# First softmax's weights of five sequences: transposed by VectorE in 32x32 blocks and by transfers within SBUF, in place of TensorE

## The chip, the core and the metric

One core of a Trainium2 chip runs the whole program. A core has TensorE (PE: matrix products, and transposes as products with an identity matrix), VectorE (DVE), ScalarE (ACT) and GpSimd (POOL). Each of them, and SyncE (SP), which in this kernel issues every transfer, works through a program of its own in a fixed order, and semaphores make one wait for another. Sixteen DMA engines move the data. Operands lie in SBUF, which has 128 partitions; products come out in the eight banks of PSUM. The metric is the time of one execution on the device, in microseconds (us).

## The reference

Eight sequences (B=8) of 576 positions, with eight heads of 64 elements, go through two softmax attentions by way of 32 packed rows for each head, and then through a channel mix with d_model = 512 and d_ff = 1024:

```python
p_packed = sm_attn(p, k, v)             # weights: 32 x 576 for each head
out = sm_attn(q, p_packed, p_packed)    # weights: 576 x 32
x = out.transpose(0, 2, 1, 3).reshape(B, S, H * D)
xk = mu_k * x + (1.0 - mu_k) * x_prev   # x_prev: the position before
xr = mu_r * x + (1.0 - mu_r) * x_prev
k = np.maximum(xk @ w_k, 0.0)
v = k * k @ w_v
r = 1.0 / (1.0 + np.exp(-(xr @ w_r)))
return r * v
```

All of it is float32. The first softmax's weights, p against k, come out with the 4 x 32 packed rows of four heads on the partitions and the 576 positions along the free axis. For the product with v the positions have to lie on the partitions, so these weights must be transposed. That step is what the change is about.

## The kernel before, in words

**Channel mix.** The 4608 rows are taken in nine blocks of 512. Each block has 48 products for the gate (`gates`, L862 to L864), 96 for the keys (`keys`, L822 to L824) and 96 for the values (`values`, L891 to L893), each 128 x 128 by 512. The operands are split into a high and a low part, so that three products stand for one. These 2160 products form the bulk of TensorE's work.

**Attention** of the sequences runs in the gaps of the channel mix, about one sequence ahead of the block that needs it. For a sequence b, `front(b)` multiplies p by k (L465, "the scores"), and `weights_of` takes each half h of the heads (0 or 1) through the first softmax: the maximum on VectorE (L540), its scaled negative (L542), and the exponential on ScalarE (L546) into the tile `a`. Five transposes on TensorE (four at L556, one at L557) turn `a` into a PSUM bank of the pool `pa`, and ScalarE copies the bank to `aT` in SBUF (L562, L564). Then `front` multiplies with v (L489, twenty products for each half; this document calls them the products with v), normalises on VectorE (L504), and `back` does the second softmax on VectorE and ScalarE and the product at L632. `mixed_in` and `mix` make the channel mix's operands of it.

**Buffers.** There is one slot for `aT`, so the second half can't write its weights before the first half's products with v are done. `e` has two slots, which `back` uses for the second softmax. `vt` has two slots for v. Before, v's first 512 positions lie in `vt` and the last 64 in `vl`. `raw` has three slots for q and k as they come in, and `kq` has four for their transposed form.

**What sets the order.** Each of these steps is a generator. `Flow` holds a planned time for every engine; each step states its engine and an estimated cost, and `Flow.run` always takes the step that can start first by the plan, then the one of better rank. That decides the order of the instructions on every engine when the program is built. On the chip nothing is moved any more: an engine whose next instruction isn't ready waits, and what stands behind it waits too. The plan's transfers are `load`: an issue on the queue (SP), a time on the DMA engines, and `LANDS` = 2.0 until the data may be used. From the third sequence on (b of 2 and more) q and k come in with position t*18 + tb in column tb*32 + t, for VectorE's 32x32 block transposes (L366). The sequences are b = 0 to 7; the change touches b = 3 to 7.

Of the kernel before, what the change touches and what calls it, by code (L numbers as in the profile page):

```python
# [8 lines left out]
F32 = mybir.dt.float32  # L9
# [154 lines left out]
def attn_pack_channel_mix(ctx: ExitStack, tc: tile.TileContext, q, k, v, p, mu_k, mu_r, w_k, w_v, w_r, out):  # L164
    nc = tc.nc
    B, H, S, D = q.shape
    NP = p.shape[2]
    DM, DF = w_k.shape
    P = 128
    NG = H // 4  # L170
    NPR = H // 2
    HS = S // 2
    NTB = S // 32
    NQ = 4 * P
# [9 lines left out]
    flow = Flow()  # L184
# [5 lines left out]
    def vec(n, after=None):  # L190
        return "vector", 0.07 + 1.04e-3 * n, after, None
# [4 lines left out]
    def act(n, after=None, table=None):  # L196
        return "scalar", 0.14 + 0.72e-3 * n, after, table
# [4 lines left out]
    def pe(us, after=None):  # L202
        return "tensor", us, after, None

    def load(dst, src, issue, us):
        yield "queue", issue, None, None
        nc.sync.dma_start(dst, src)
        begin = max(flow.free.get("dma", 0.0), flow.t + 0.46)
        flow.free["dma"] = begin + us
        flow.free["queue"] = max(flow.free["queue"], begin - 2.0)  # L210
        flow.now.t = begin + us + LANDS
# [5 lines left out]
    def reached():  # L217

        yield None, 0.0, None, None

    EARLY = 2

    const = ctx.enter_context(tc.tile_pool(name="const", bufs=1))
# [8 lines left out]
    def tile_(shape, dtype, tag, slot, name=None):  # L232
        return sb.tile(shape, dtype, name=name or tag, tag=f"{tag}{slot}")

    def banks(slot):
        return ps.tile([P, 2, 512], F32, name="pa", tag=f"pa{slot}")
# [5 lines left out]
            const.tile([P, 1 if "m" == tag[0] or "n" == tag[0] else 2], F32, name=f"{tag}{j}", tag=f"{tag}{j}")  # L242
    for tag, n, size in (
        ("xk", NC, 2 * TB), ("sq", NF, 2 * TB), ("tmp", 4, WP), ("sig", 4, DM), ("kq", 4, S), ("a", 2, S),
        ("raw", 3, S), ("a2", 1, S), ("e", 2, S), ("aT", 1, 5 * P), ("vt", 2, NPR * 4 * D),
    ):
        for j in range(n):
            sb.tile([P, size], F32, name=tag, tag=f"{tag}{j}")
# [51 lines left out]
    ts, vts, pts, xts, xt2 = {}, {}, {}, {}, {}  # L300

    def rank(b, n=0):

        return (10 if b == 0 else RANK_1 if b == 1 else 30) + 0.1 * (2 * b + n)
# [4 lines left out]
    def loads(b):  # L309
        flow.spawn(packed(b), lrank(b) - (0.03 if b else 0.015))  # L310
        for src, tag in ((k, "kT"), (v, "vt"), (q, "qT")):
# [8 lines left out]
            for pr in range(NPR):  # L320

                space = "xk" if b == 0 else "raw"
                slot = yield from flow.take(space)
                if b < EARLY:

# [21 lines left out]
    def back_to_issue():  # L347
        flow.now.t = flow.free["queue"]

    def values_of(b, h):  # L350

        slot = yield from flow.take("vt")
        vt = tile_([P, NPR, 4 * D], F32, "vt", slot)
        vl = tile_([S - NQ, NPR, D], F32, "vl", slot)
        yield from load(vt, v[b, h::2, :NQ, :].rearrange("h (p c) d -> p h (c d)", c=4), 0.46, 1.8)
        back_to_issue()
        yield from load(vl, v[b, h::2, NQ:, :].rearrange("h p d -> p h d"), 0.63, 0.45)
        vts[b, h] = slot, vt, vl
        flow.set(("vt", b, h))

    def transposed(tag, b, pr, raw_slot, raw):
# [86 lines left out]
    def two_slots():  # L448

        lock = yield from flow.take("both")  # L450
        first = yield from flow.take("pa")
        second = yield from flow.take("pa")
        flow.give("both", lock)
        return first, second

    def front(b):

        yield from flow.wait(("pt", b), *(("kT", b, pr) for pr in range(NPR)))
        slots = yield from two_slots()
        yield pe(1.2)  # L460
        s1 = [banks(slot) for slot in slots]
        for hf in range(2):
            for pr in range(NPR):
                for h, own in enumerate(HALVES):
                    nc.tensor.matmul(  # L465
                        s1[h][32 * pr:32 * pr + 32, hf, :HS], pts[b][1][own, pr, :],
                        ts["kT", b, pr][1][own, hf * HS:(hf + 1) * HS],
                        start=True, stop=True,
                    )
        for pr in range(NPR):  # L470
            flow.give("kq", ts.pop(("kT", b, pr))[0])
        flow.give("pt", pts.pop(b)[0])
        sm = const.tile([P, 2], F32, name="sm", tag=f"sm{b % 2}")
        for h in range(2):
            flow.spawn(weights_of(b, h, slots[h], s1[h], sm), rank(b) + 0.01 * h)

        yield from flow.wait(("aT", b, 0))
        slot = yield from flow.take("pa")
        pv = banks(slot)
        for h in range(2):  # L480
            yield from flow.wait(("aT", b, h), ("vt", b, h))
            yield pe(0.55)
            sv, vt, vl = vts.pop((b, h))
            sT, aT = aTs.pop((b, h))
            for c in range(5):
                n = P if c < 4 else S - NQ
                for pr in range(NPR):
                    own = slice(32 * pr, 32 * pr + 32)
                    nc.tensor.matmul(  # L489
                        pv[own, h, :D], aT[:n, c, own], vt[:, pr, c * D:(c + 1) * D] if c < 4 else vl[:, pr, :],  # L490
                        start=(c == 0), stop=(c == 4),
                    )
            flow.give("aT", sT)
            flow.give("vt", sv)
        summed = flow.t
        rs = const.tile([P, 2], F32, name="rs", tag=f"rs{b % 2}")
        yield vec(2, after=0.0)
        nc.vector.tensor_scalar_add(rs, sm, eps)
        yield vec(20)
        nc.vector.reciprocal(rs, rs)  # L500
        sp = yield from flow.take("pm")
        pm = tile_([P, 2, D], F32, "pm", sp)
        yield vec(P, after=max(flow.t, summed))
        nc.vector.tensor_tensor(pm, pv[:, :, :D], rs.unsqueeze(2).broadcast_to([P, 2, D]), op=ALU.mult)  # L504
        flow.give("pa", slot)

        slot = yield from flow.take("pa")
        yield pe(0.21)
        pT = banks(slot).rearrange("p a b -> p (a b)")
        nc.tensor.transpose(pT[:, :P], pm.rearrange("p a b -> p (a b)"), ident)  # L510
        ppT = sb.tile([P, P], F32, name="ppT", tag="ppT")
        yield act(P)
        nc.scalar.copy(ppT, pT[:, :P])
        flow.give("pa", slot)
        left = [2]
        first = None
        if b == 0:
            sx = yield from flow.take("xt")

            a2 = tile_([P, 2, S + 1], F32, "xt", sx, "a2t")  # L520
            nc.gpsimd.memset(a2[:, :, 0:1], 0.0)
            first = dict(a2=(sx, a2), left=4)
            flow.spawn(shared(ppT, first), RANK_MIX - 0.1)
        for hf in range(2):
            flow.spawn(back(b, hf, sp, pm, ppT, left, first), rank(b, hf) - 1)

    aTs = {}

    def in_order(b, natural, blocks, x):

        if b < EARLY:
            return natural, x[:, :, :HS]
        return blocks, x[:, :, :HS].rearrange("p a (b t) -> p a b t", t=32)

    def weights_of(b, h, slot, s1, sm):

        mx = const.tile([P, 1], F32, name="mx", tag=f"mx{h}")
        nmx = const.tile([P, 1], F32, name="nmx", tag=f"nmx{h}")
        yield vec(S)
        nc.vector.tensor_reduce(mx, s1[:, :, :HS], axis=AX.XY, op=ALU.max)  # L540
        yield vec(1)
        nc.vector.tensor_scalar_mul(nmx, mx, -scale)  # L542
        sa = yield from flow.take("a")
        a = tile_([P, S], F32, "a", sa)
        yield act(S + 320 if b < EARLY else 2 * S + 220, table="exp")
        nc.scalar.activation(  # L546
            *in_order(b, a.rearrange("p (a s) -> p a s", a=2), a.rearrange("p (t a b) -> p a b t", a=2, t=32), s1),
            AF.Exp, bias=nmx, scale=scale, accum_out=sm[:, h:h + 1],
        )
        flow.give("pa", slot)  # L550

        slot = yield from flow.take("pa")
        yield pe(0.65)
        tp = banks(slot).rearrange("p a b -> p (a b)")
        for c in range(4):
            nc.tensor.transpose(tp[:, c * P:(c + 1) * P], a[:, c:NQ:4], ident)  # L556
        nc.tensor.transpose(tp[:S - NQ, NQ:NQ + P], a[:, NQ:], ident)  # L557
        flow.give("a", sa)
        sT = yield from flow.take("aT")
        aT = tile_([P, 5, P], F32, "aT", sT)  # L560
        yield act(NQ)
        nc.scalar.copy(aT[:, :4, :], tp[:, :NQ].rearrange("p (a b) -> p a b", b=P))  # L562
        yield act(P, after=0.0)
        nc.scalar.copy(aT[:S - NQ, 4, :], tp[:S - NQ, NQ:NQ + P])  # L564
        flow.give("pa", slot)
        aTs[b, h] = sT, aT
        flow.set(("aT", b, h))

# [74 lines left out]
    def mixed_in(b, hf, g, slot, px):  # L643
# [8 lines left out]
        xt = xt2[b, g][1]  # L652
        yield act(S if b < EARLY else 2 * S)
        nc.scalar.copy(*in_order(
# [334 lines left out]
```

## Time and profile before

| | |
|---|---|
| three executions | 603.91, 605.03, 605.74 us; median 605.03 us |
| the profiled execution | 605.65 us, of which the span from its first to its last instruction is 603.9 us |
| matrix products for the weights' transposes of b = 3 to 7 | 50 of TensorE's instructions in the program |
| ScalarE's copy of the transposed weights, L562 and L564 | 586 ns and 256 ns, for each half of each sequence |
| VectorE's 32x32 block transpose of a 128 x 576 tile, L366 | 754 to 765 ns |
| transfers issued by SP | 354 |

The profile's page gives for each engine the busy time, then the span in 40 slices, the queues, the chain of work that ended last, and groups of instructions by line. A matrix product's duration is the time that it spends in a pipeline; successive products overlap, so the distance between the starts of two of them says what one costs, and the duration doesn't. The trace counts a float32 product of the attention twice (two passes), so that L465's 16 products appear as x32.

### The profile page before, as it was taken

The numbers are of one execution on the slowest core, as the hardware profiler recorded it, in microseconds if no ns is written. First come the engines' busy times: TensorE is split into PE (matmuls) and PEld (weight loads), VectorE is DVE, ScalarE is ACT, GpSimd is POOL, SyncE is SP. The second block draws the span as 40 slices with busy tenths as digits, with TensorE's granted clock in tenths as the row PEclk, the third lists the DMA queues.
The fourth block names the chain that finished last, engine by engine and source line by source line (L and its number), as shares of the span: only waits on it lengthen the run. The fifth ranks groups of instructions, "written<-read, shape, count | busy, mean of one in ns | idle before, by whom it ended". The sixth has DMA issues, their size and how long they took to land.

```text
span 603.9 us, 10289 instructions
## 1 busy us (share of the span) xinstructions
PE 592.3 (98%) x4024; PEld 466.1 (77%) x4024; DVE 361.8 (60%) x702; ACT 324.5 (54%) x578; POOL 2.1 (0%) x22
## 2 busy tenths in 40 slices
PE   8899999999999999999999999999999999999997
PEld 8675777777777777777877787778788888888886
DVE  2499989949688489456856576267403812541321
ACT  4457793775674758454945484458434703631410
POOL 0000000000000000000000000000000000000000
PEclk9899999999999999999999999999999999999999
DMA  8679560765535645446034602000000010001001
GB/s 235 170 216 297 179 146 3 177 120 120 88 50 150 106 76 117 116 77 139 2 101 75 137 0 78 13 1 0 35 37 0 1 71 1 0 1 69 1 1 69
DMA packets 159312, 49.43 MB, mean 82 GB/s; under 512 B 143904, under 2 KB 152096, under 8 KB 159264
## 3 DMA queue, kind: packets, MB, share of 16 engines
q1 hardware_dynamic: 159264, 48.79, 33.8%
q8 instruction: 31, 0.51, 0.3%
q14 instruction: 17, 0.14, 0.1%
HBM read 39.33 MB, written 9.44 MB: 81 GB/s over the span
## 4 chain that ended last, share of the span: by engine, by line
PE 86%; DVE 5%; ACT 3%; DMA 3%; issue 1%; SPq 1%
PE pvo L891 11%; PE ph L822 11%; PE pvo L892 10%; PE pvo L893 10%; PE ph L823 10%; PE ph L824 10%; PE pr L862 5%; PE pr L863 5%; PE pr L864 5%; PE pa L489 2%; PE pa L577 2%; PE pa L632 2%; DMA vt<-in_v 1%; PE pa L465 1%; PE pa L556 1%
## 5 line engine op out<-in xcount | busy, mean ns | idle before, releaser
L822 PE MATMUL ph<-xk,wk_h 128*128 128x512 f32 x288 | 115.0, 399 | 0.0
L891 PE MATMUL pvo<-wv_h,sq 128*128 128x512 f32 x288 | 113.9, 396 | 0.0
L823 PE MATMUL ph<-xk,wk_h 128*128 128x512 f32 x288 | 112.7, 391 | 1.1 <-DVE xk L729 1.1
L824 PE MATMUL ph<-xk,wk_l 128*128 128x512 f32 x288 | 112.4, 390 | 0.0
L892 PE MATMUL pvo<-wv_l,sq 128*128 128x512 f32 x288 | 112.3, 390 | 0.0
L893 PE MATMUL pvo<-wv_h,sq 128*128 128x512 f32 x288 | 112.2, 390 | 0.0
L840 DVE CAST sq<-r 128x512 fp32r<-128x512 f32 x72 | 30.2, 420 | 99.2 <-ACT r L836 98.6
L833 ACT ACTIVATE r<-ph 128x512 f32<-128x512 f32 x72 | 43.0, 597 | 86.7 <-PE ph L824 85.8
L822 PEld LDWEIGHTS ph<-xk,wk_h 128*128 128x128 f32 x288 | 54.1, 188 | 16.1 <-issue 4.5
L891 PEld LDWEIGHTS pvo<-wv_h,sq 128*128 128x128 f32 x288 | 54.1, 188 | 16.0 <-issue 4.5
L823 PEld LDWEIGHTS ph<-xk,wk_h 128*128 128x128 f32 x288 | 54.2, 188 | 12.4 <-DVE xk L729 2.3
L893 PEld LDWEIGHTS pvo<-wv_h,sq 128*128 128x128 f32 x288 | 54.1, 188 | 11.4
L824 PEld LDWEIGHTS ph<-xk,wk_l 128*128 128x128 f32 x288 | 54.1, 188 | 11.4
L892 PEld LDWEIGHTS pvo<-wv_l,sq 128*128 128x128 f32 x288 | 54.1, 188 | 10.7
L862 PE MATMUL pr<-wr_h,xr 128*128 128x512 f32 x144 | 58.9, 409 | 0.0
L863 PE MATMUL pr<-wr_l,xr 128*128 128x512 f32 x144 | 56.4, 392 | 0.5 <-DVE wr_l L296 0.5
L787 DVE SCALAR_TENSOR_TENSOR x<-xt,mus,x 128x64 f32<-128x64 f32 (+7 forms) x120 | 53.9, 498 | 4.2 <-ACT x L783 4.1
L864 PE MATMUL pr<-wr_h,xr 128*128 128x512 f32 x144 | 56.3, 391 | 0.0
L783 ACT ACTIVATE x<-xt,mus 128x64 f32<-128x64 f32 (+7 forms) x120 | 54.5, 514 | 0.2 <-DVE xr L805 0.2
L873 ACT ACTIVATE sig<-pr 128x512 f32<-128x512 f32 x36 | 21.3, 601 | 61.6 <-PE pr L864 58.0
L842 DVE TENSOR_TENSOR sq<-r,sq 128x512 fp32r<-128x512 f32 x72 | 49.4, 686 | 1.6
L902 DVE TENSOR_TENSOR sig<-pvo,sig 128x512 f32<-128x512 f32 x36 | 23.8, 686 | 42.3 <-PE pvo L893 42.3
(95 smaller groups left out, 720.5 us busy)
## 6 DMA issues: line engine op xcount, KB each, us to landing
out<-sig SPq DMA_DIRECT2D x36, 256.0 KB, 2.1
vt<-in_v SPq DMA_DIRECT2D x16, 512.0 KB, 5.3
raw<-in_q SPq DMA_DIRECT2D x112, 72.0 KB, 2.8
raw<-in_k SPq DMA_DIRECT2D x96, 72.0 KB, 2.8
st<-in_moe_w_k SPq DMA_DIRECT2D x8, 512.0 KB, 6.0
st<-in_moe_w_v SPq DMA_DIRECT2D x8, 512.0 KB, 5.5
raw<-in_k SPq DMA_DIRECT2D x16, 144.0 KB, 3.1
st<-in_moe_w_r SPq DMA_DIRECT2D x4, 512.0 KB, 5.2
```

The lines of the kernel that those rows point to most:

```text
L783: nc.scalar.mul(x32[:, o:o + n], xts[b, c][:, 1 + s:1 + s + n], mus[:, j, c:c + 1])
L787: nc.vector.scalar_tensor_tensor(x32[:, o:o + n], xts[b, c][:, s:s + n], mus[:, j + 1, c:c + 1], x32[:, o:o + n], op0=ALU.mult, op1=ALU.add,)
L822: nc.tensor.matmul(ph, wk_h[:, c, fs], xh, start=(c == 0), stop=False)
L823: nc.tensor.matmul(ph, wk_h[:, c, fs], xl, start=False, stop=False)
L824: nc.tensor.matmul(ph, wk_l[:, c, fs], xh, start=False, stop=(c == NC - 1))
L842: nc.vector.tensor_tensor(hl[:, 1, :], r, hl[:, 0, :].bitcast(F32), op=ALU.subtract)
L862: nc.tensor.matmul(pr, xh[:, ts_], wr_h[:, c, :], start=(c == 0), stop=False)
L863: nc.tensor.matmul(pr, xh[:, ts_], wr_l[:, c, :], start=False, stop=False)
L864: nc.tensor.matmul(pr, xl[:, ts_], wr_h[:, c, :], start=False, stop=(c == NC - 1))
L891: nc.tensor.matmul(pv[t], sh, wv_h[:, f, :], start=(f == 0), stop=False)
L892: nc.tensor.matmul(pv[t], sh, wv_l[:, f, :], start=False, stop=False)
L893: nc.tensor.matmul(pv[t], sl, wv_h[:, f, :], start=False, stop=(f == NF - 1))
```

## The change

For b of 3 and more (`MOVED = 3`), the five transposes on TensorE and ScalarE's two copies are gone for each half of the heads. In their place, `weights_moved` takes a slot of `e`, has VectorE transpose `a` in 32x32 blocks (one instruction, 128 x 576) into the tile `blocks`, and issues sixteen transfers on SP from `blocks` to `aT`. Each of them moves 32 partitions by four or five blocks of 32 numbers (512 or 640 bytes for each partition): for each of the four pairs of heads pr, and for each of four groups j of 32 partitions of `aT`, a run of positions (`RUNS`). ScalarE's exponential now writes `a` in natural order. The sum over positions is arranged anew, so v is loaded for these sequences in four transfers for each half instead of two, with the same runs. For b below 3 only the tile of v's last 64 positions changes: it lies in `vt` now.

```diff
+    RUNS = (0, 5), (5, 5), (10, 4), (14, 4)
+    MOVED = 3
...
-        vl = tile_([S - NQ, NPR, D], F32, "vl", slot)
-        yield from load(vt, v[b, h::2, :NQ, :].rearrange("h (p c) d -> p h (c d)", c=4), 0.46, 1.8)
...
+            own = v[b, h::2].rearrange("h (t tb) d -> t h (tb d)", tb=NTB)
+            for j, (first, n) in enumerate(RUNS):
+                yield from load(vt[32 * j:32 * j + 32, :, :n * D], own[:, :, first * D:(first + n) * D], 0.46, 0.5)
...
-                        pv[own, h, :D], aT[:n, c, own], vt[:, pr, c * D:(c + 1) * D] if c < 4 else vl[:, pr, :],
+                        pv[own, h, :D], aT[:n, pr, c] if b >= MOVED else aT[:n, c, own], vt[:n, pr, c * D:(c + 1) * D],
...
+        natural = a.rearrange("p (a s) -> p a s", a=2)
+        yield act(S + 320 if b < EARLY or b >= MOVED else 2 * S + 220, table="exp")
...
+        if b >= MOVED:
+            yield from weights_moved(b, h, sa, a)
+            return
...
+    def weights_moved(b, h, sa, a):
+
+        se = yield from flow.take("e")
+        blocks = tile_([P, NTB, NP], F32, "e", se, "blocks")
+        yield vec(S)
+        nc.vector.transpose(blocks, a.rearrange("p (k t) -> p k t", t=32))
+        flow.give("a", sa)
+        sT = yield from flow.take("aT")
+        aT = tile_([P, NPR, 5, NP], F32, "aT", sT)
+        for pr in range(NPR):
+            for j, (first, n) in enumerate(RUNS):
+                own = slice(32 * pr, 32 * pr + 32)
+                yield from load(aT[32 * j:32 * j + 32, pr, :n], blocks[own, first:first + n], 0.45, 0.06)
+                if (pr, j) != (NPR - 1, 3):
+                    back_to_issue()
+        flow.give("e", se)
+        aTs[b, h] = sT, aT
+        flow.set(("aT", b, h))
```

Since `Flow` sets the order from its costs, everything behind the fourth sequence's weights stands in another order. Two places show it. The first is TensorE's program at b = 5, before: the gate's products (L862 to L864) around the two halves' transposes (L556, L557) and the first half's products with v (L489).

```order
L864 MATMUL pr<-wr_h,xr 128x512
L556 MATMUL pa<-ident,a 128x128 x4
L557 MATMUL pa<-ident,a 64x128
L556 MATMUL pa<-ident,a 128x128 x4
L557 MATMUL pa<-ident,a 64x128
L862 MATMUL pr<-wr_h,xr 128x512
L863 MATMUL pr<-wr_l,xr 128x512
L864 MATMUL pr<-wr_h,xr 128x512
L489 MATMUL pa<-vt,aT 32x64 x16
L489 MATMUL pa<-vl,aT 32x64 x4
L862 MATMUL pr<-wr_h,xr 128x512
```

The same engine at b = 5 with the change, at the second half: the products with v (now L500) stand alone among the values' products (now L926 to L928).

```order
L926 MATMUL pvo<-wv_h,sq 128x512
L927 MATMUL pvo<-wv_l,sq 128x512
L928 MATMUL pvo<-wv_h,sq 128x512
L500 MATMUL pa<-vt,aT 32x64 x20
L926 MATMUL pvo<-wv_h,sq 128x512
L927 MATMUL pvo<-wv_l,sq 128x512
L928 MATMUL pvo<-wv_h,sq 128x512
```

The transposes are gone, and more of the channel mix's products stand between the scores, the first half's products with v and the second half's. Counted in the changed program's order:

| sequence b | 128x512 products between the scores and the first half's products with v | groups of L632 among them | 128x512 products between the two halves |
|---|---|---|---|
| 3 | 72 | 1 | 60 |
| 4 | 66 | 1 | 48 |
| 5 | 72 | 1 | 48 |
| 6 | 81 | 1 | 48 |
| 7 | 81 | 2 | 45 |

The second place is SP's program at b = 5. Before, the sixteen loads of q are followed by the next sequence's p (`pin`) and k, with four stores of results between.

```order
L207 DMA raw<-in_q 32x18x32 x16
L207 DMA pin<-in_p 32x4x32
L207 DMA out<-sig 128x512 x4
L207 DMA pin<-in_p 32x4x32 x3
L207 DMA raw<-in_k 32x18x32 x16
```

With the change, the first half's sixteen transfers (`aT<-blocks`) stand behind the loads of q; behind them come p and three of the sixteen loads of k, and then the second half's.

```order
L207 DMA raw<-in_q 32x18x32 x16
L207 DMA aT<-blocks 32x160 x2
L207 DMA aT<-blocks 32x128 x2
L207 DMA aT<-blocks 32x160 x2
L207 DMA aT<-blocks 32x128 x2
L207 DMA aT<-blocks 32x160 x2
L207 DMA aT<-blocks 32x128 x2
L207 DMA aT<-blocks 32x160 x2
L207 DMA aT<-blocks 32x128 x2
L207 DMA pin<-in_p 32x4x32 x4
L207 DMA raw<-in_k 32x18x32 x3
L207 DMA aT<-blocks 32x160 x2
```

At the other sequences the loads between the two halves' transfers are seven of k (b = 3, where four stores also stand among the second half's transfers), two of p and five of k (b = 4), four of p and three of k (b = 6), and none (b = 7). SP issues 534 transfers in all with the change, 354 before.

More of the change, by code (lines that the diff above doesn't have):

```diff
@@ L244, in attn_pack_channel_mix @@
         ("xk", NC, 2 * TB), ("sq", NF, 2 * TB), ("tmp", 4, WP), ("sig", 4, DM), ("kq", 4, S), ("a", 2, S),
-        ("raw", 3, S), ("a2", 1, S), ("e", 2, S), ("aT", 1, 5 * P), ("vt", 2, NPR * 4 * D),
+        ("raw", 3, S), ("a2", 1, S), ("e", 2, S), ("aT", 1, 5 * P), ("vt", 2, NPR * 5 * D),
     ):
@@ L352, in values_of @@
         slot = yield from flow.take("vt")
-        vt = tile_([P, NPR, 4 * D], F32, "vt", slot)
-        vl = tile_([S - NQ, NPR, D], F32, "vl", slot)
-        yield from load(vt, v[b, h::2, :NQ, :].rearrange("h (p c) d -> p h (c d)", c=4), 0.46, 1.8)
-        back_to_issue()
-        yield from load(vl, v[b, h::2, NQ:, :].rearrange("h p d -> p h d"), 0.63, 0.45)
-        vts[b, h] = slot, vt, vl
+        vt = tile_([P, NPR, 5 * D], F32, "vt", slot)
+        if b < MOVED:
+            yield from load(
+                vt[:, :, :4 * D], v[b, h::2, :NQ, :].rearrange("h (p c) d -> p h (c d)", c=4), 0.46, 1.8
+            )
+            back_to_issue()
+            yield from load(vt[:S - NQ, :, 4 * D:], v[b, h::2, NQ:, :].rearrange("h p d -> p h d"), 0.63, 0.45)
+        else:
+            own = v[b, h::2].rearrange("h (t tb) d -> t h (tb d)", tb=NTB)
+            for j, (first, n) in enumerate(RUNS):
+                yield from load(vt[32 * j:32 * j + 32, :, :n * D], own[:, :, first * D:(first + n) * D], 0.46, 0.5)
+                if j < 3:
+                    back_to_issue()
+        vts[b, h] = slot, vt
         flow.set(("vt", b, h))
@@ L482, in front @@
             yield pe(0.55)
-            sv, vt, vl = vts.pop((b, h))
+            sv, vt = vts.pop((b, h))
             sT, aT = aTs.pop((b, h))
@@ L544, in weights_of @@
         a = tile_([P, S], F32, "a", sa)
-        yield act(S + 320 if b < EARLY else 2 * S + 220, table="exp")
+        natural = a.rearrange("p (a s) -> p a s", a=2)
+        yield act(S + 320 if b < EARLY or b >= MOVED else 2 * S + 220, table="exp")
         nc.scalar.activation(
-            *in_order(b, a.rearrange("p (a s) -> p a s", a=2), a.rearrange("p (t a b) -> p a b t", a=2, t=32), s1),
+            *(natural, s1[:, :, :HS]) if b >= MOVED
+            else in_order(b, natural, a.rearrange("p (t a b) -> p a b t", a=2, t=32), s1),
             AF.Exp, bias=nmx, scale=scale, accum_out=sm[:, h:h + 1],
@@ L565, in weights_of @@
         flow.give("pa", slot)
+        aTs[b, h] = sT, aT
[13 more added lines that the diff above has]
+                if (pr, j) != (NPR - 1, 3):
+                    back_to_issue()
+        flow.give("e", se)
         aTs[b, h] = sT, aT
```

## The prediction

> **What bounds the kernel now.** I read the page's shares and its chain of work first, then the busy time in stretches, then TensorE's waits.
>
> ```profile
> span 603.9 us, 10289 instructions
> PE 592.3 (98%) x4024; PEld 466.1 (77%) x4024; DVE 361.8 (60%) x702; ACT 324.5 (54%) x578; POOL 2.1 (0%) x22
> PE 86%; DVE 5%; ACT 3%; DMA 3%; issue 1%; SPq 1%
> ```
>
> ```profile
> 210.00:240.00 30.00, 30.00 (x221) 23.10 (x214) 27.40 (x58) 19.55 (x39) 0.20 (x2) 1.00 0.52 99
> 240.00:270.00 30.00, 30.00 (x273) 22.37 (x272) 16.25 (x30) 14.33 (x21) 0.00 (x0) 1.00 0.45 91
> ```
>
> ```profile
> PE pq L421 <- DMA raw<-in_q: 2.3, 1, 2.3
> PE pa L489 <- ACT aT L564: 0.5, 2, 0.3
> ```
>
> TensorE is busy for 98% of the span and carries 86% of the chain. In the stretch that the change touches it is busy for all of each 30 us (second column), at a granted clock of 1.00, and its waits for the weights come to 0.5 us in all. So a product taken off TensorE there is time off the end, and a wait put on it there is time onto the end. Work added to VectorE or SP costs only what it makes TensorE wait.
>
> **What is removed: TensorE's time.** A product's cost is the distance between starts. First b = 5, where both halves' transposes stand together; b = 3, 6 and 7 have the same pair of rows.
>
> ```profile
> 254.01 0.39 PE L863 MATMUL pr<-wr_l,xr 128*128 128x512 f32 x1
> 254.24 0.40 PE L864 MATMUL pr<-wr_h,xr 128*128 128x512 f32 x1
> 254.47 0.63 PE L556 MATMUL pa<-ident,a 128*128 128x128 f32 x4
> ...
> 255.88 0.39 PE L863 MATMUL pr<-wr_l,xr 128*128 128x512 f32 x1
> ```
>
> Without the transposes L863 would start two distances of 0.23 us behind L864's 254.24, at 254.70. It starts at 255.88, so a pair of halves costs 1.18 us. At b = 4 the halves stand apart:
>
> ```profile
> 205.67 0.39 PE L824 MATMUL ph<-xk,wk_l 128*128 128x512 f32 x1
> 205.99 0.75 PE L556 MATMUL pa<-ident,a 128*128 128x128 f32 x4
> ...
> 206.92 0.40 PE L823 MATMUL ph<-xk,wk_h 128*128 128x512 f32 x1
> ...
> 207.85 0.40 PE L824 MATMUL ph<-xk,wk_l 128*128 128x512 f32 x1
> 208.08 0.63 PE L556 MATMUL pa<-ident,a 128*128 128x128 f32 x4
> ...
> 208.90 0.39 PE L823 MATMUL ph<-xk,wk_h 128*128 128x512 f32 x1
> ```
>
> By the same rule (1.25 - 0.46) + (1.05 - 0.46) = 1.38 us. **Removed: 4 x 1.18 + 1.38 = 6.1 us.** The group's mean of 290 ns for a transpose would give twice that, but it counts the overlap. ScalarE's copies and the PSUM bank are also freed. That is worth nothing by itself: these copies' cost on TensorE is within the 0.5 us above.
>
> **What is added: a chain from the scores to the products with v.** SP's issue distance c is the number that matters, since sixteen issues stand in a row, twice for each sequence. No transfer within SBUF is in this trace. The nearest rows are SP's:
>
> ```profile
> 161.01 2.04 SPq L207 DMA_DIRECT2D pin<-in_p  x4
> 163.16 3.27 SPq L207 DMA_DIRECT2D raw<-in_k  x5
> 251.08 1.84 SPq L207 DMA_DIRECT2D out<-sig  x4
> ```
>
> ```profile
> out<-sig SPq DMA_DIRECT2D x36, 256.0 KB, 2.1
> ```
>
> ```profile
> L207 SPq DMA_DIRECT2D raw<-in_k x112: 312/630/1432, 0.7 to 329.9; - x112
> L207 SPq DMA_DIRECT2D out<-sig x36: 332/332/1305, 116.7 to 600.9; - x36
> L207 SPq DMA_DIRECT2D pin<-in_p x32: 422/430/706, 5.7 to 310.7; - x32
> ```
>
> The distance is 0.46 us for the stores, 0.51 for loads with 32 partitions of four pieces, 0.65 for loads with 32 partitions of eighteen pieces. From an issue's start to landing takes 2.1 us for a store. A moved transfer has 32 partitions and one piece in each. It is nearest to the store, which also has one piece for each partition, and has a quarter of its pieces; I take c = 0.44, a little under the store. The last three rows have the issues alone (lowest, median and highest ns): 430 ns of the 0.51 for `pin`, so that 0.08 us lies between two issues. The bounds are 0.41 (the store's 332 ns and 0.08) and 0.65. With landing as for the store, the chain from the first issue to the last landing is 15 x 0.44 + 2.1 = **8.7 us** (8.3 to 11.9).
>
> **First half: from the end of the scores.** What stands ahead of the transfers I read from where TensorE's transposes could start before; the plan placed those too when the weights were ready.
>
> ```profile
> 154.05 1.20 PE L465 MATMUL pa<-kT,pt 64*32 64x288 f32 x32
> 165.05 0.63 PE L556 MATMUL pa<-ident,a 128*128 128x128 f32 x4
> 199.20 1.20 PE L465 MATMUL pa<-kT,pt 64*32 64x288 f32 x32
> 245.72 1.20 PE L465 MATMUL pa<-kT,pt 64*32 64x288 f32 x32
> 304.46 1.20 PE L465 MATMUL pa<-kT,pt 64*32 64x288 f32 x32
> 315.46 0.63 PE L556 MATMUL pa<-ident,a 128*128 128x128 f32 x4
> 366.82 1.20 PE L465 MATMUL pa<-kT,pt 64*32 64x288 f32 x32
> 379.18 0.63 PE L556 MATMUL pa<-ident,a 128*128 128x128 f32 x4
> ```
>
> From the end of the scores to the transposes: 9.8, 5.6, 7.6, 9.8 and 11.2 us for b = 3 to 7. To this comes VectorE's block transpose, 0.77 us by the row below, and the exponential is 0.60 us shorter in natural order, as the first two sequences have it (first row) against the later ones (second row).
>
> ```profile
> L546 ACT ACTIVATE a<-pa,nmx x4: 727/736/741, 14.5 to 76.0; 128x576 f32<-128x576 f32 x4
> L546 ACT ACTIVATE a<-pa,nmx x8: 1328/1340/1343, 204.6 to 374.0; 128x576 f32<-128x576 f32 x8
> L366 DVE STREAM_TRANSPOSE qT<-raw 128x576 f32<-128x576 f32 x24 | 17.9, 765 | 18.2 <-PE pa L465 9.9 <-DMA raw<-in_q 8.1
> ```
>
> So the need is these numbers plus 0.2 plus 8.7: 18.7, 14.5, 16.5, 18.7, 20.1 us. The cover is what stands between on TensorE in the changed order: 72, 66, 72, 81 and 81 large products at 0.226 us, with one group of L632 (two at b = 7) at about 0.9 with its gap.
>
> ```profile
> 480.00:540.00 60.00, 60.00 (x266) 49.71 (x266) 24.26 (x41) 22.23 (x37) 0.00 (x0) 1.00 0.05 18
> ```
>
> ```profile
> 192.04 0.67 PE pa L632 x16
> ```
>
> 60.00 us for 266 products is the 0.226. The cover is 17.2, 15.8, 17.2, 19.2 and 20.1 us. Only b = 3 falls short, by 1.5 us; the others come out at 0 to 1.3 us to spare. SP gives the same for b = 3: before, the first load of the next k is issued at 163.16, 7.9 us behind the scores' end at 155.25; four more loads of v (at 0.51) and that load of k put the first transfer at 10.6 us.
>
> **Second half: from the first half's products with v.** `aT` has one slot, so SP's first transfer of the second half waits for those products, and everything behind it on SP (loads for the next sequence, stores) waits with it. Loads that stand ahead of it delay it further. Seven loads of k at b = 3 last 0.44 + 7 x 0.65 = 5.0 us, against the 2.1 us of landing and 0.9 of the products with v (the row below, with its gap), so the transfers start 2.0 us late; b = 4 gives 1.7, b = 5 and 6 give 1.4, b = 7 none.
>
> ```profile
> 128.55 0.83 PE pa L489 x40
> ```
>
> The need is then 2.0 + 8.7 + 1.8 (four stores among them) = 12.5, 10.4, 10.1, 10.1 and 8.7 us; the cover is 60, 48, 48, 48 and 45 products: 13.6, 10.8, 10.8, 10.8 and 10.2 us. **No wait at c = 0.44, with 0.4 to 1.5 us to spare.** At c = 0.51 each need grows by 1.05 us: the first halves wait 2.6 (b = 3), 0.4, 0.6 and 1.1 (b = 5 to 7), the second halves 0.7, 0.4 and 0.4 (b = 4 to 6), 6 us in all.
>
> **Other edits.** Ten block transposes add 7.7 us to VectorE between 150 and 390 us, where its fullest stretch above is 27.40 of 30 us: they fit, with little room at 210 to 240; uncovered there, two would cost 1.5 us. v's loads in four pieces give SP eight issues for the former four, 8 x 0.51 = 4.1 us, far ahead of use but for b = 3. The memory added in `vt` costs no time.
>
> **A rule against the change.** The transposes that leave TensorE took 0.58 us for five, as the rows above show, while the path that takes their place takes 8.7 us by SP's rows. The Trainium skill, "VectorE: DVE Perf Modes", section "Rules for kernel authors", advises TensorE for a 128x128 transpose when PSUM may be the destination, as it could here. The trace agrees on latency, but that price is paid on an engine that is full; whether the rule decides the time hangs on the cover alone, and it is the third case below.
>
> **The sum.** On the profiled execution: 605.65 - 6.1 + 1.5 = 601.05 us. Its time lies 0.6 above the median of 605.03, so on the median this is 600.4.
>
> **The rivals.**
> 1. *The waits eat the gain.* c is 0.48 to 0.52, or VectorE and ScalarE reach the weights 1 us later than before. For it: seven of the ten places have under 1 us to spare by my own rows. Against it: the order was placed with such costs, and the present order, placed the same way, makes TensorE wait only 0.5 us for weights. With waits of 4 to 7 us it gives 603 to 606.
> 2. *SP becomes the bound: slower.* If a transfer within SBUF issues like the loads of eighteen pieces, c = 0.65, each need grows by 3.2 us. First halves wait 4.7 + 1.9 + 2.5 + 2.7 + 3.2, second halves 2.1 + 2.8 + 2.5 + 2.5 + 1.7: 26.6 us, so 605.03 - 6.1 + 26.6 = 625.5. SP would also fill: for one sequence 32 loads at 0.65, 8 of v and 4 of p at 0.51, 4.5 stores at 0.46 and 32 transfers at 0.65 are 50 us, where b = 4 to b = 5 has 183 large products, 41 us, plus some 6 us of small ones. It decides from about c = 0.53, where the waits by the same sums reach 8 us. Against it: the pieces are few, and the fastest loads above issue in 312 ns, though they have many. This is the case in which the rule of the Trainium skill above would hold.
> 3. *VectorE is the late one* at its full stretch: two more instructions for each sequence hold up the operands of the channel mix, 1.5 us each time, 7.7 at most: 600 to 607. It mixes with the first rival.
>
> That the transposes stay is no case: the order has them out.
>
> **How the numbers follow.** Forecast, waits of 0 to 3.6 us, so 598.9 to 602.5: 0.62. First and third rival, 602.5 to 607: 0.21, about a quarter of it under 603.2. SP as the bound, 607 to 630: 0.17. The predicted time is the forecast's, 600.4. The range goes from no waits at all (605.03 - 6.1 = 598.9, less 0.2) up to 606.0 for c = 0.51 and some more; what lies above has under 2 in 10. A measurement of this kernel can tell about 0.3%, 1.8 us, from no change. Faster by over that is under 603.2: 0.62 and a quarter of 0.21, 0.67. Slower is over 606.8: 0.17 and a little, 0.18. Between: 0.15.
>
> **What would show it.** The start distance of the sixteen transfers on SP (0.41 to 0.46 for the forecast), and their landing (about 2.1); TensorE's waits at the products with v, which should be 1 to 2 us in all, mostly at b = 3's first half; VectorE's block transposes at 0.77 us. L556's x64 should be x24. If TensorE waits longer than 6 us there, the forecast is wrong; if SP's transfers stand at over 0.53, the second rival is right; if the waits come at the channel mix's operands instead, the third.

## The result, and the profile after

| | before | after |
|---|---|---|
| median of four executions | 605.02 us | 627.80 us |
| lowest and highest | 603.91 and 605.74 us | 626.25 and 630.62 us |
| profiled execution, its span | 605.65, 603.9 us | 630.62, 628.8 us |
| mean granted clock of the profiled execution | 0.996 | 0.977 |

The ratio is 1.0382 (95% interval 1.0352 to 1.0412): slower by 22.8 us, where 4.6 us less was forecast. The 627.8 lies outside the predicted range, 2.3 us above the second rival's 625.5.

The page of after, first its span, TensorE's row (busy time, share, instructions) with those of the others, the granted clock in 40 slices, and the shares of the chain of work:

```profile
span 628.8 us, 10479 instructions
PE 601.5 (96%) x3974; PEld 469.5 (75%) x3974; DVE 369.1 (59%) x712; ACT 310.8 (49%) x556; POOL 2.1 (0%) x22
...
PEclk9799999999989999998999899979999999999999
...
PE 55%; SPq 21%; DVE 11%; DMA 6%; issue 4%; ACT 3%; DVEq 0%; ACTq 0%
```

TensorE runs 50 instructions fewer, as it should, and yet is busy 9 us longer. The chain, 86% TensorE before, now goes through SP's queue for 21%. Some slices have a clock of 8 or 7 tenths; that is the largest part of the longer busy time, and comes back below. Two further views say where SP comes in: TensorE's waits (total, number, longest in us), and SP's issues of the transfers (lowest, median and highest ns).

```profile
PE pa L500 <- DMA aT<-blocks: 16.8, 10, 2.4
```

```profile
L207 SPq DMA_DIRECT2D aT<-blocks x160: 507/589/1440, 164.4 to 424.2; - x160
```

Nine of the ten groups of products with v (now L500) wait for the moved weights, one of them twice, 16.8 us in all, where the waits for weights had been 0.5 us. One issue takes 589 ns, not the 0.36 that a distance of 0.44 us allows. SP's timeline for b = 3 (start, length in us) gives the distance itself:

```profile
163.72 0.57 SPq L207 DMA_DIRECT2D raw<-in_k  x1
164.39 10.07 SPq L207 DMA_DIRECT2D aT<-blocks  x16
174.50 5.28 SPq L207 DMA_DIRECT2D raw<-in_k  x7
179.89 8.80 SPq L207 DMA_DIRECT2D aT<-blocks  x14
188.79 2.00 SPq L207 DMA_DIRECT2D out<-sig  x4
190.84 1.15 SPq L207 DMA_DIRECT2D aT<-blocks  x2
```

Sixteen transfers take 10.07 us: **c is 10.07 / 16 = 0.63 us**. The page's landings of the same transfers (issues, KB, median us from issue to landing) are:

```profile
aT<-blocks SPq DMA_DIRECT2D x80, 20.0 KB, 1.8
aT<-blocks SPq DMA_DIRECT2D x80, 16.0 KB, 1.8
```

So the last weights of b = 3's first half land at 164.39 + 15 x 0.63 + 1.8 = 175.6 us. TensorE's timeline at that place (start, length; in brackets the idle time ahead):

```profile
172.74 0.39 PE L928 MATMUL pvo<-wv_h,sq 128*128 128x512 f32 x1
173.06 0.46 PE L500 MATMUL pa<-vt,aT 128*32 128x64 f32 x6
175.88 0.85 PE L500 MATMUL pa<-vt,aT 128*32 128x64 f32 x34 [2.36 <-DMA aT<-blocks]
176.66 0.50 PE L926 MATMUL pvo<-wv_h,sq 128*128 128x512 f32 x1
177.00 0.44 PE L927 MATMUL pvo<-wv_l,sq 128*128 128x512 f32 x1
177.23 0.63 PE L928 MATMUL pvo<-wv_h,sq 128*128 128x512 f32 x1
177.66 0.63 PE L926 MATMUL pvo<-wv_h,sq 128*128 128x512 f32 x1
...
180.22 0.58 PE L926 MATMUL pvo<-wv_h,sq 128*128 128x512 f32 x1
180.64 0.39 PE L927 MATMUL pvo<-wv_l,sq 128*128 128x512 f32 x1
180.87 0.39 PE L928 MATMUL pvo<-wv_h,sq 128*128 128x512 f32 x1
```

Two costs are to be read here.

**The wait.** The first six of the forty rows (a product is counted twice) start, the rest wait until 175.88, a quarter of a microsecond behind the landing. From the last large product ahead (172.74) to the first behind (176.66) it is 3.92 us; without a wait that distance is 1.16 us (before, at four of five sequences, and in the changed kernel where nothing is late). So 2.76 us are lost.

**The clock.** From 177.23 to 180.22 the large products start 0.43 us apart, then again 0.23. Eight cost 0.2 us more each, 1.6 us in all. The same rows stand behind five of the ten waits. In stretches (second column TensorE's busy time, third from the end the granted clock) the wait and the clock are seen together:

```profile
165.00:180.00 15.00, 12.64 (x85) 9.96 (x85) 11.67 (x26) 10.60 (x25) 0.20 (x2) 0.91 0.30 54
405.00:420.00 15.00, 12.43 (x77) 9.50 (x77) 2.21 (x4) 3.06 (x5) 0.00 (x0) 0.77 0.10 25
```

The Trainium skill, "TensorE: Matmul & The Clock Gate", Part 1, has a gate that halves the array's clock after an idle window of some 3.4 us and gives it back after some 3.4 us of work. On the way back the trace agrees roughly: the eight products of 0.43 us here are 3.4 us, and the slow stretches behind the four other waits last 3.0 to 4.9 us. On the idle window it doesn't: the longest of the waits is 2.4 us.

Read in this way for all ten places (us):

| | b = 3 | 4 | 5 | 6 | 7 | sum |
|---|---|---|---|---|---|---|
| first half, lost at the products with v | 2.8 | 2.7 | 2.0 | 2.2 | 3.6 | 13.3 |
| second half, lost | 1.2 | 3.6 | 1.6 | 1.2 | 0.0 | 7.5 |
| slow products behind them | 1.6 | 1.2 | 1.6 | 1.6 | 2.3 | 8.3 |

The spans differ by 24.9 us. Of these, -6.1 (TensorE's removed products), -0.2 (the wait of before at b = 3), +20.8 and +8.3 make 22.8; about 2 us of this execution are not assigned. The other three executions of after have a mean clock of 0.988 to 0.991 and take 2 to 4 us less, so the share of the slow products differs from one execution to the next.

What the change added to VectorE costs what the prediction had, by the groups of after (count, busy us, mean ns, idle ahead):

```profile
L590 DVE STREAM_TRANSPOSE blocks<-a 128x576 f32<-128x576 f32 x10 | 7.4, 764 | 1.3 <-ACT a L558 1.2
```

### The profile page after: what moved, and what is told of

Same layout as the page of the kernel before. It is cut to its first block, busy times and chain, and to the rows that moved or that the text cites. A ratio compares the mean times of both kernels' runs of the same rounds, so it can differ in the third digit from the quotient of the medians.

```text
span 628.8 us, 10479 instructions
## 1 busy us (share of the span) xinstructions
PE 601.5 (96%) x3974; PEld 469.5 (75%) x3974; DVE 369.1 (59%) x712; ACT 310.8 (49%) x556; POOL 2.1 (0%) x22
## 4 chain that ended last, share of the span: by engine, by line
PE 55%; SPq 21%; DVE 11%; DMA 6%; issue 4%; ACT 3%; DVEq 0%; ACTq 0%
SPq L207 21%; PE pvo L926 7%; PE pvo L927 7%; PE pvo L928 7%; PE ph L857 6%; PE ph L858 6%; PE ph L859 6%; PE pr L897 3%; PE pr L898 3%; PE pr L899 3%; DMA raw<-in_q 2%; DMA vt<-in_v 2%; PE pa L612 2%; DMA aT<-blocks 2%; PE pa L500 1%
## 5 line engine op out<-in xcount | busy, mean ns | idle before, releaser
L857 PE MATMUL ph<-xk,wk_h 128*128 128x512 f32 x288 | 117.5, 408 | 0.0
L858 PE MATMUL ph<-xk,wk_h 128*128 128x512 f32 x288 | 114.8, 399 | 1.1 <-DVE xk L764 1.1
L926 PE MATMUL pvo<-wv_h,sq 128*128 128x512 f32 x288 | 115.1, 400 | 0.7 <-ACT r L868 0.7
L859 PE MATMUL ph<-xk,wk_l 128*128 128x512 f32 x288 | 114.2, 397 | 0.0
L928 PE MATMUL pvo<-wv_h,sq 128*128 128x512 f32 x288 | 113.3, 393 | 0.0
L857 PEld LDWEIGHTS ph<-xk,wk_h 128*128 128x128 f32 x288 | 55.4, 192 | 17.4 <-issue 5.2
L926 PEld LDWEIGHTS pvo<-wv_h,sq 128*128 128x128 f32 x288 | 54.6, 190 | 17.2 <-issue 4.7
L858 PEld LDWEIGHTS ph<-xk,wk_h 128*128 128x128 f32 x288 | 55.5, 193 | 12.8 <-DVE xk L764 2.2
L859 PEld LDWEIGHTS ph<-xk,wk_l 128*128 128x128 f32 x288 | 55.4, 192 | 11.9
L928 PEld LDWEIGHTS pvo<-wv_h,sq 128*128 128x128 f32 x288 | 54.6, 190 | 11.7
L897 PE MATMUL pr<-wr_h,xr 128*128 128x512 f32 x144 | 57.7, 401 | 0.0
L899 PE MATMUL pr<-wr_h,xr 128*128 128x512 f32 x144 | 56.0, 389 | 0.0
```

The lines of the kernel that those rows point to most:

```text
L857: nc.tensor.matmul(ph, wk_h[:, c, fs], xh, start=(c == 0), stop=False)
L858: nc.tensor.matmul(ph, wk_h[:, c, fs], xl, start=False, stop=False)
L859: nc.tensor.matmul(ph, wk_l[:, c, fs], xh, start=False, stop=(c == NC - 1))
L897: nc.tensor.matmul(pr, xh[:, ts_], wr_h[:, c, :], start=(c == 0), stop=False)
L899: nc.tensor.matmul(pr, xl[:, ts_], wr_h[:, c, :], start=False, stop=(c == NC - 1))
L926: nc.tensor.matmul(pv[t], sh, wv_h[:, f, :], start=(f == 0), stop=False)
```

## The experiments

The theory: **the change as such gains its 6 us, and loses 29 because the order on TensorE was placed for transfers that issue in 0.45 us, while they take 0.63.** The rivals: SP is full and would be late in any order; the moved path is too long for any cover; the halved clock is most of it; the transposes were worth less than 6.1 us.

### What the removed products were worth

Before, with the transposes of b = 3 to 7 left out and nothing in their place (ScalarE copies the weights as they lie):

```diff
+        if b >= 3:
...
+            nc.scalar.copy(aT[:, :4, :], a[:, :NQ].rearrange("p (a b) -> p a b", b=P))
...
+            return
```

> This is the kernel before in which b = 3 to 7 leave the transposition of the first softmax's weights out: ScalarE's copies take them untransposed from SBUF, so the output isn't the reference's. No transfer is added. It measures the term of 6.1 us by itself. If the transposes cost TensorE what the distances between starts say: 605.0 - 6.1 = 598.9 us (598.3 to 600). If their place was partly free (other work would have waited there anyway): 601 to 605.

597.55 us against 606.03, ratio 0.9878 (0.9843 to 0.9914): by the ratio 7.4 us less, interval 5.2 to 9.5. The prediction's 6.1 lies in it. This is about what the change could win, if the moved path cost nothing.

### The same transfers, placed for what they cost

After, with one number of the plan changed; the kernel issues the same 160 transfers:

```diff
-                yield from load(aT[32 * j:32 * j + 32, pr, :n], blocks[own, first:first + n], 0.45, 0.06)
+                yield from load(aT[32 * j:32 * j + 32, pr, :n], blocks[own, first:first + n], 0.63, 0.06)
```

> The changed kernel with one number of the plan altered: a transfer's issue is planned at 0.63 us, as the trace of the changed kernel has it, not at 0.45. The transfers are the same; TensorE's products with v stand later in its order. Theory 'placed too early': the ten waits of 0.9 to 2.4 us fall below 5 us in all, no product runs at half the distance rate after them, and the time is 599 to 604 us. Rival 'SP is full': 32 issues of 0.63 us for each sequence don't fit between the loads, the next sequence's loads and scores come late, and the time stays above 612 us.

601.59 us against 606.03, ratio 0.9926 (0.9897 to 0.9956). The edit takes the change from 3.8% slower to 0.7% faster. In its trace the transfers issue in the same time, by SP's issues:

```profile
L207 SPq DMA_DIRECT2D aT<-blocks x160: 507/588/1382, 161.8 to 412.5; - x160
```

and TensorE's waits have no row for them any more. What is left there at the products with v is of sequences that still go by ScalarE:

```profile
PE pa L500 <- ACT aT L580: 0.5, 1, 0.5
```

The wait at b = 3 that was 2.36 us is gone, in TensorE's timeline:

```profile
173.89 0.90 PE L500 MATMUL pa<-vt,aT 128*32 128x64 f32 x40
174.72 0.50 PE L926 MATMUL pvo<-wv_h,sq 128*128 128x512 f32 x1
175.06 0.40 PE L927 MATMUL pvo<-wv_l,sq 128*128 128x512 f32 x1
```

All forty rows, twenty products, go without a gap, and behind them the large ones are at full clock. Between the two halves' products with v now stand 72, 69, 60, 60 and 57 large products, where after has 60, 48, 48, 48 and 45. So the wait was one of order. "SP is full" falls, and so does "too long for any cover": the same work on SP makes TensorE wait next to nothing (0.5 us lost at the ten places) when it is asked for later.

The same kernel once more, with more executions:

> e2_true_cost once more with five rounds, on the chip of the other two: 0.993 of the kernel before, by its first interval 0.990 to 0.996.

601.21 us against 605.57, ratio 0.9937 (0.9913 to 0.9961).

### How the time goes with the planned issue

Two more values of the same number, run beside that repeat, 0.54 and, in a second kernel, 0.72:

```diff
-                yield from load(aT[32 * j:32 * j + 32, pr, :n], blocks[own, first:first + n], 0.45, 0.06)
+                yield from load(aT[32 * j:32 * j + 32, pr, :n], blocks[own, first:first + n], 0.54, 0.06)
```

> The changed kernel with the transfer's issue planned at 0.54 us, halfway between 0.45 and 0.63. The products with v stand some 15 x 0.09 = 1.35 us later than in the changed kernel, at ten places. If the loss is the shortfall of the plan at each place (20.8 us of waits at 0.45), some 8 us of waits are left, and the time is 604 to 612 us. If any wrong plan costs as much: 620 and more.

> The issue planned at 0.72 us, more than the 0.63 it takes. The products with v stand where the weights have long come: no waits there. If lateness costs nothing while the attention is still ahead of the channel mix: 599 to 603, as e2_true_cost. If the attention then falls behind: waits at the gates' or keys' operands, 605 to 615.

| planned issue, us | time | ratio to before (95%) | lost at the ten places | slow products |
|---|---|---|---|---|
| 0.45 (after) | 627.80 | 1.0382 (1.0352 to 1.0412) | 20.8 | 8.3 |
| 0.54 | 614.45 | 1.0152 (1.0122 to 1.0182) | 14.2 | 2.9 |
| 0.63 | 601.21 | 0.9937 (0.9913 to 0.9961) | 1.3 (0.5 in the first trial) | 0 |
| 0.72 | 598.35 | 0.9887 (0.9863 to 0.9910) | -0.1 | 0 |

At 0.54 I had expected 604 to 612 and got more. Half of the error in c takes away only a third of what is lost. The first halves lose 6.3 us in place of 13.3, but the second halves 8.0 in place of 7.5, although six more large products, 1.4 us, stand ahead of each. Two things in the traces work against them. Behind the first halves of b = 3, 5 and 6 no slow products lie any more, which had been 1.6 us of cover each. And the plan's other steps move too: at b = 5, seven loads of k (5.3 us) stand ahead of the second half's transfers, where after has four of p and three of k (4.0 us). At 0.72, over the true cost, the time is lowest, a little under the 599 to 603 that I expected, and it is the best version found; its ratio is, within the intervals, that of the kernel with the transposes left out. Its page:

```profile
span 596.7 us, 10467 instructions
PE 586.7 (98%) x3974; PEld 460.0 (77%) x3974; DVE 366.4 (61%) x712; ACT 312.1 (52%) x558; POOL 2.1 (0%) x22
```

### The order kept, the chain shortened

The other way round: TensorE's program row for row that of after, but eight issues in place of sixteen for each half, each for two head pairs (the second pair's own weights aren't moved). The plan still counts sixteen at 0.45.

```diff
-                yield from load(aT[32 * j:32 * j + 32, pr, :n], blocks[own, first:first + n], 0.45, 0.06)
+                yield from load(
+                    None if pr % 2 else aT[32 * j:32 * j + 32, pr:pr + 2, :n],
...
+                    else blocks[own, NTB - 2 * n:].rearrange("p (two n) s -> p two n s", two=2), 0.45, 0.06,
+                )
```

> The changed kernel with eight transfers of the same bytes in all for each half instead of sixteen: each fills two pairs of heads of aT from one pair's weights, so the second pair's weights are left out and the output isn't the reference's. The plan still counts sixteen issues, so TensorE's program is the changed kernel's, row for row. Theory 'the sixteen issues of 0.63 us make the weights late': eight last 7 x 0.63 + 1.8 = 6.2 us against 11.3, under every cover, the ten waits go, and the time is 598 to 601 us. Rival 'the changed order itself is bad (second softmax, mixes and loads stand worse)': above 610 us, with waits elsewhere.

599.48 us against 605.22, ratio 0.9897 (0.9875 to 0.9918); -0.1 us lost at the ten places. SP's timeline at b = 3:

```profile
161.94 0.57 SPq L208 DMA_DIRECT2D raw<-in_k  x1
162.60 5.16 SPq L208 DMA_DIRECT2D aT<-blocks  x8
167.81 4.64 SPq L208 DMA_DIRECT2D raw<-in_k  x7
172.80 5.85 SPq L208 DMA_DIRECT2D aT<-blocks  x8
```

5.16 us for eight, half of after's 10.07, with nearly the same distance (0.645). With the order untouched, shortening SP's chain alone removes the whole loss. Together with the last two this pins the cause from both sides, chain and cover. What then remains, 0.9887 and 0.9897, is within the intervals what leaving the transposes out gives, so no other part of the change costs much.

A version that moves all weights with few issues goes by HBM: one transfer out, four back.

```diff
...
+        yield from load(held[h], blocks, 0.45, 0.9)
+        back = held[h].rearrange("(pr t) k n -> t pr k n", pr=NPR)
+        for j, (first, n) in enumerate(RUNS):
+            yield from load(aT[32 * j:32 * j + 32, :, :n], back[:, :, first:first + n], 0.5, 0.3)
...
```

> The changed kernel with the move made through HBM: one transfer writes a half's blocks (128 x 576) to HBM, and four bring them back, each with 32 partitions and all four pairs of heads: five issues for each half instead of sixteen. By rows, the issues last 0.41 + 4 x 0.49 us, the write lands in about 2.1 and the reads in 3 to 4: some 8 us, of which SP is held for 2.4 instead of 10. If it is the number of issues within SBUF that costs, TensorE has no waits at the products with v and the time is 598 to 602, as with the plan set right. If HBM's round trip is later than planned (3.3 us for each leg), waits come back: 605 to 615.

600.57 us against 605.22, ratio 0.9929 (0.9898 to 0.9960), and 1.25 us lost at the ten places. It does no better than sixteen transfers placed rightly.

### The clock by itself

After, with nine products of the identity by itself ahead of each group of products with v, so that TensorE is at work while it would wait:

```diff
+            if b >= MOVED:
+                for _ in range(9):
+                    nc.tensor.matmul(pv[:, h, 128:256], ident, ident, start=True, stop=True)
```

> The changed kernel with nine idle products (identity by identity, 128x128, about 0.22 us each, into an unused part of the bank) ahead of each of the ten groups of products with v for b = 3 to 7. They wait for nothing, so TensorE works for 2.0 us in which it only waited. The weights come no sooner. Theory 'the waits also halve the clock': no large products at a distance of 0.43 us behind the groups, and 6 to 9 us less than the changed kernel's 627.8: 619 to 622. Rival 'the loss is all in the waits': the time stays at 627 to 630.

625.96 us against 606.03, ratio 1.0329 (1.0301 to 1.0357). The 619 to 622 that I expected was missed. The first place again, in TensorE's timeline:

```profile
172.39 0.39 PE L931 MATMUL pvo<-wv_h,sq 128*128 128x512 f32 x1
172.62 2.17 PE L496 MATMUL pa<-ident 128*128 128x128 f32 x18
174.71 0.31 PE L503 MATMUL pa<-vt,aT 128*32 128x64 f32 x6
175.35 0.85 PE L503 MATMUL pa<-vt,aT 128*32 128x64 f32 x34 [0.33 <-DMA aT<-blocks]
```

The idle products fill most of the wait, no product at 0.43 us is left, and the run's mean clock is 0.994. But lost at the ten places, with the idle products, are now 26.2 us in place of 20.8, and 26.2 against 29.1 is near what the time shows (the ratios differ by 0.005, with touching intervals). Where the clock stays up, the second half's products with v come earlier, but its weights, paced by SP, don't: the second halves lose 2.5, 3.4, 2.3, 2.9 and 2.0 us, 13.1 in place of 7.5, while the first halves lose 13.1 in place of 13.3. The 2.0 at b = 7 are the idle products alone, for nothing is waited for there. So 3.4 us of the 8.3 that the slow products took (26.2 - 2.0 - 20.8) were under the cover of SP's next chain. The halved clock follows from the waits. By these sums it adds some 4.9 us of its own (29.1 - 24.2), an estimate that the times don't resolve; it is not most of the loss.

### What sets the length of an issue

Before, with 36 transfers of six shapes behind its end, six of each in a row (one execution; only the issues are read from it):

```diff
+        many("rowsA", "sq1", 6, lambda d, i: d[part(i), :160], lambda i: src[part(i + 1), :160])
+        many("rowsB", "sq2", 6, lambda d, i: d[:, 160 * i:160 * i + 160], lambda i: src[:, 160 * i:160 * i + 160])
...
+        many("rowsD", "sq4", 6, lambda d, i: d[part(i), :64], lambda i: v[0, 0, 32 * i:32 * i + 32, :])
```

> The kernel before with 36 transfers more behind its last store, in six groups of six, into SBUF that nothing uses any more; its time grows by the 15 to 25 us that they last and tells nothing. What is read is the length of one issue on SP. rowsA: 32 partitions of 160 numbers within SBUF, as the change has them (0.59 us there). rowsB: 128 partitions of 160 within SBUF. rowsC: 32 partitions of 640. rowsD: 32 partitions of 64, out of HBM. rowsE: as rowsA, but to the same partitions. rowsF: 64 partitions of 160. If the source within SBUF makes it slow: A, B, C, E and F at 0.55 to 0.60, D at 0.33 to 0.43. If the 32 partitions do: A, C, D and E slow, B and F at about 0.33 as the stores. If the crossing to other partitions does: E at 0.33 to 0.43.

SP's issues (lowest, median, highest ns): A is the moved transfer's shape, B has 128 partitions, C four times the bytes, D comes from HBM, E stays on its partitions, F has 64 partitions.

```profile
L970 SPq DMA_DIRECT2D rowsA<-src x6: 534/578/589, 600.3 to 603.5; - x6
L970 SPq DMA_DIRECT2D rowsB<-src x6: 532/597/601, 604.1 to 607.3; - x6
L970 SPq DMA_DIRECT2D rowsC<-src x6: 534/588/597, 607.9 to 611.2; - x6
L970 SPq DMA_DIRECT2D rowsD<-in_v x6: 365/414/570, 611.8 to 614.3; - x6
L970 SPq DMA_DIRECT2D rowsE<-src x6: 513/590/591, 614.7 to 617.8; - x6
L970 SPq DMA_DIRECT2D rowsF<-src x6: 461/480/594, 618.5 to 622.8; - x6
```

Neither four times the partitions nor four times the bytes, nor staying on the partitions, changes the issue by more than 20 ns. What A, B, C and E share is SBUF as source and as target; D with the same 32 partitions, from HBM, takes 414 ns. F at 480 doesn't fit; its issues stood further apart, and why is open. Nor is SBUF at both ends the only case of a long issue. The version by HBM writes `held` from SBUF to HBM, and these writes, of 128 partitions with 2304 bytes each, issue in 620 ns at the median, where the stores of results, also from SBUF to HBM, take 332 to 356:

```profile
L207 SPq DMA_DIRECT2D held<-blocks x10: 376/620/1447, 163.0 to 374.6; - x10
```

So what sets the length of an issue isn't settled; that these transfers take 0.63 us is.

### One sequence more

The change for b = 2 too (`MOVED = 2`), on the kernel planned with 0.63 and on the one by HBM:

```diff
-    MOVED = 3
+    MOVED = 2
```

> The kernel of e2_true_cost with MOVED = 2, so that the third sequence's transposes leave TensorE too (six sequences). Two groups of five transposes are 1.2 us: 600.4 against e2's 601.6 if SP still has room at b = 2, where the weights' conversion has just ended. If b = 2's transfers come late behind the loads: 603 to 608.

> e6_bounce with MOVED = 2: 0 to 2 us below e6_bounce, 597 to 601, if e6 has no waits.

610.86 us, ratio 1.0083 (1.0063 to 1.0104), and 606.25 us, ratio 1.0013 (0.9994 to 1.0033): both slower than with five sequences, not faster. TensorE's waits, first of the former, then of the latter:

```profile
PE pr L897 <- ACT xr L838: 7.5, 2, 5.2
PE pa L500 <- DMA aT<-blocks: 0.5, 2, 0.2
```

```profile
PE pr L899 <- DVE xr L840: 4.0, 2, 2.4
```

The weights are in time, but now the gate's operands are late. Probably the attention has less slack, one sequence earlier, to the block that needs it, and the longer path takes it; the slack wasn't measured by itself. So what the path may cost seems to hang on the place in the program.

## Why the prediction was wrong

- **The bound, and the removed 6.1 us: right.** Three kernels without waits at these places, by three ways, come, by their ratios, to 6.2 to 7.4 us less than before (no transposes 0.9878, eight issues 0.9897, planned with 0.72 0.9887).
- **VectorE's transposes: right.** 764 ns each, as its transpose of q, and hidden; TensorE has no wait for VectorE that would be the third rival's.
- **Landing, 2.1: mis-sized, with little weight.** It is 1.8 us. The store that I took it from moves 256 KB and ends in HBM; these move 16 to 20 KB and end in SBUF. Size has a part in it: the shapes B and C, 80 KB within SBUF, land in 2.0 us.
- **"It is nearest to the store, which also has one piece for each partition, and has a quarter of its pieces; I take c = 0.44": this step failed.** It took the number of pieces for what sets an issue's length. The shapes show that it isn't, in this range: transfers within SBUF issue in 578 to 597 ns in four of five shapes, with 32 pieces as with 128. What does set it stays open, and no row of before was of a transfer within SBUF. c is 0.63, close to the upper bound of 0.65. I had both ends on record, but gave the upper one 0.17; nothing in the trace stood nearer to the one than to the other, for all rows had HBM at one end.
- **The sums of need and cover: right in kind, and nearly in size.** With c = 0.63 and a landing of 1.8 each need grows by 15 x 0.19 - 0.3 = 2.55 us. The first halves then wait 4.1, 1.3, 1.9, 2.1 and 2.6 us, the second 1.5, 2.2, 1.9, 1.9 and 1.1: 20.1 in all before rounding, where 20.8 was lost. Single places are off by up to 1.5 us, in both directions, so the total agrees better than its parts.
- **That a wait costs only its own length: partly wrong.** The sum has no term for slow products. The clock halves behind five of the ten waits, 8.3 us in this execution. By the trial with idle products, 3.4 us of this stood where SP would have made TensorE wait anyway.
- **The second rival: its price near (625.5 against 627.8), in part by luck, and one of its reasons wrong.** It counts 26.6 us of waits, where 20.8 were lost, and none of the 8.3 for slow products; the two errors nearly cancel. It had SP full as well. SP issues the same transfers without a wait once they are asked for later (0.63, 0.72). The bound is the chain of sixteen issues against its cover, not SP's total. It was said to decide from about c = 0.53; at 0.63 it has decided, and nearer than that nothing was tried.
- **The rule of the Trainium skill for transposes** ("VectorE: DVE Perf Modes", "Rules for kernel authors") agrees with the result as it stands, but not as a rule about this change: planned with 0.72, the path that avoids TensorE is faster by 1.1%.
- **The chances.** Seven of the ten places had under 1 us to spare, by my own sums, and sixteen issues multiply any error in c by fifteen. An unknown with that lever, whose bounds reach from a gain of 6 us to a loss of 20, should not have had 0.62 on one end.

Not tried: a second slot for `aT`, so that the second half's transfers need not stand behind the first half's products; and one transfer for all four head pairs within SBUF.

## What to carry to other kernels

Where a planner orders the program, an operation's planned cost is part of the change: measure a new kind of transfer before it is planned, and when in doubt enter it too long. Here 0.09 us too long cost nothing, and 0.18 us too short, sixteen times in a row, turned a gain of 1% into a loss of 4%. If a chain of n issues has to be covered, the error in one issue counts n times, so a slack of a microsecond is none.

## What the hardware showed

- On SP, a transfer from SBUF to SBUF issued in 0.58 to 0.61 us at the median, back to back about 0.63 apart, with 32 or 128 partitions and 512 to 2560 bytes in each; the shape with 64 partitions (F) in 0.48. One from HBM (D) took 0.41, a store of results to HBM 0.33 (its row of before), a write of `held` to HBM 0.62. From issue to landing it was 1.8 us for the moved weights and 2.1 for a store.
- A wait of TensorE of under 2.4 us can be followed by 5 to 11 large products at half rate, 0.43 us apart. Which waits do this can't be told from their length: behind the one of 1.76 us at 289.1 us seven products were slow, behind the one of 2.19 us at 232.4 us none. TensorE's timeline at both:

```profile
232.39 0.85 PE L500 MATMUL pa<-vt,aT 128*32 128x64 f32 x34 [2.19 <-DMA aT<-blocks]
233.18 0.50 PE L926 MATMUL pvo<-wv_h,sq 128*128 128x512 f32 x1
233.51 0.39 PE L927 MATMUL pvo<-wv_l,sq 128*128 128x512 f32 x1
233.74 0.40 PE L928 MATMUL pvo<-wv_h,sq 128*128 128x512 f32 x1
...
289.10 0.85 PE L500 MATMUL pa<-vt,aT 128*32 128x64 f32 x34 [1.76 <-DMA aT<-blocks]
289.88 0.80 PE L857 MATMUL ph<-xk,wk_h 128*128 128x512 f32 x1
290.48 0.63 PE L858 MATMUL ph<-xk,wk_h 128*128 128x512 f32 x1
290.91 0.63 PE L859 MATMUL ph<-xk,wk_l 128*128 128x512 f32 x1
```
